# Retention plus channel mix on one core: the first q block in halves of the heads, v of block 1 ahead of its k, and a new hand order

## The chip, the core and the metric

The kernel runs on one core of a Trainium2 chip. The metric is device time in microseconds (us). Each engine of the core (PE for matmuls, DVE, ACT, POOL, and SP, which here only issues transfers) runs its own list of instructions in order and waits at semaphores for the others.

## The reference, cut to what matters

Two layers follow each other. The first is a linear recurrence for each of 4 batches and 8 heads (768 tokens, 64 values a head); the second mixes each token with the one before it and runs a gated network of three weight matrices (512x1024, 1024x512, 512x512).

```python
gamma = 1.0 - 2.0 ** (-5.0 - np.arange(H))
for t in range(S):
    state = gamma * state + einsum('bhd,bhe->bhde', k[:, :, t], v[:, :, t])
    y[:, :, t] = scale * einsum('bhd,bhde->bhe', q[:, :, t], state)
x = y.transpose(0, 2, 1, 3).reshape(B, S, H * D)
xk = mu_k * x + (1 - mu_k) * x_prev          # x_prev: x one token earlier
xr = mu_r * x + (1 - mu_r) * x_prev
k = maximum(xk @ w_k, 0); v = k * k @ w_v; r = sigmoid(xr @ w_r)
out = r * v
```

## The kernel before, in words

The tokens are cut into 12 blocks of 256 (`TM`), three to a batch; a block is two chunks `u` of 128. Heads are taken in pairs `j` (four of them). Everything is written as a string `ORDER` of words such as `S.1.0@23`: a code, its block and further numbers, and after `@` the banks of PSUM that the result goes to (eight banks, 0 to 7). The program walks through the string and emits the functions of the codes; there is no scheduler, so the string alone fixes the order of the instructions of each engine. Waits follow from the data, from the reuse of PSUM banks and from the rings of buffers (four each for q, v and k, three for the scaled k, five for the output tiles).

The codes, with the engine and the line of the profile before:

- Loads. `lq`, `lv` (POOL queue, L175; they cast to 16 bits), `lk.n` (SP queue), `lk.n.2` (POOL queue), `wk.h`, `wv.h`, `wr` (POOL queue, L510, L517, L513; a half of w_k, a half of w_v, the whole of w_r, 512 KB each as stored). `mu` loads two small vectors over ACT's queue.
- Retention. `ks` scales k (L188; `.0` on DVE, `.1` on POOL). `T` turns k (PE L203, 8 instructions); `Tq` turns q and `Tk` turns k in 32 small instructions into two banks (PE L221). `E.n.0` copies the turned q, `E.n.1` the turned k (ACT L249). `S.n.i` scores (PE L257), `M.n.i` masks them (DVE L264), `C` makes the new state (PE L282), `U` adds it up (DVE L294, L298), `G` decays it (POOL L301), `I` and `Y` make the output (PE L313, L326), `D` scales it into x (DVE L340; `Du` by chunks, L348).
- Channel mix. `dx.n.e` takes the difference to the token before (L355; e=0 on DVE, 1 on POOL); `X.n.w.j` mixes (DVE L369, w=0 for xk, 1 for xr). `K.n.g` is a quarter of the first matrix product (PE L406), `Q` squares its positive part (two ACT instructions, L413 and L416), `R.n.tb` is the gate's product (PE L420), `s` its sigmoid (ACT L426), `V.n.tb.part` half of the last product (PE L432), `O.n.tb` the output tile (DVE L438), `st.n.tb` its store (SP queue, L445).
- For block 0 the mix goes by chunks: `du`, `Xu`, `Ku` (PE L386), `Qu`. The last output tile goes by halves of its columns: `Vc` (PE L450), `Oc` (DVE L457), `sc`.
- `gy` builds a table of powers (DVE L500 to L503, eight instructions), `mt` and `me` turn and copy mu, and `z.n` is n matmuls on zeros whose result nobody reads.

As the program is built, a transfer of POOL's queue waits until the one eight places before it has landed, since the queue takes eight semaphores in turn; SP and ACT share eight more in the same way.

Of the kernel before, what the change touches and what calls it, by code (L numbers as in the profile page):

```python
# [25 lines left out]
Xu.0.1.1.2.3 s.0.0 X.1.0.3.4 R.0.1@4 E.2.1 X.1.0.2.3 X.1.0.1.2 X.1.0.0.1 Tq.2@67 s.0.1 C.2@3
X.1.1.3.4 lq.6 E.2.0 K.1.2@2 X.1.1.0.1 X.1.1.1.2 K.1.3@4 X.1.1.2.3 Q.1.2 U.2.0 G.2.0 K.1.1@5 Q.1.3
ks.3.1 S.2.0@23 I.2.0@67 M.2.0 K.1.0@4 lk.5.2 V.0.0.1 Q.1.0 lv.5 S.2.1@23 T.3.1@4 M.2.1 V.0.1.1
E.3.1 O.0.0 Y.2 Q.1.1 O.0.1 st.0.0 C.3@23 D.2 Tq.3@45 st.0.1 ks.6.1 R.1.0@0 E.3.0 U.3.0 V.1.0.0@1
U.3.1 s.1.0 G.3.1 S.3.0@23 I.3.0@45 S.3.1@67 ks.4.1 R.1.1@0 M.3.1 V.1.0.1 s.1.1 M.3.0 dx.2.1  # L30
T.4.1@0 V.1.1.0@6 O.1.0 E.4.1 st.1.0 Y.3 lk.7 lq.5 X.2.0.3.4 Tq.4@01 X.2.0.2.3 C.4@23 E.4.0
X.2.0.1.2 lv.7 V.1.1.1 X.2.0.0.1 X.2.1.2.3 lv.6 K.2.1@7 X.2.1.1.2 X.2.1.3.4 X.2.1.0.1 K.2.3@0
Q.2.1 U.4.0 D.3 G.4.0 R.2.0@7 Q.2.3 ks.5.1 K.2.0@2 U.4.1 O.1.1 s.2.0 K.2.2@3 Q.2.0 st.1.1 G.4.1
lk.10 S.4.0@67 lk.8 I.4.0@45 Q.2.2 dx.3.1 S.4.1@01 lk.9 V.2.1.0@2 M.4.1 V.2.0.0@3 M.4.0 lq.8
R.2.1@0 X.3.0.2.3 lq.7 V.2.0.1 X.3.0.1.2 s.2.1 X.3.1.0.1 V.2.1.1 X.3.1.1.2 X.3.0.0.1 X.3.1.3.4
C.5@0 Tq.5@67 X.3.0.3.4 Y.4 E.5.0 X.3.1.2.3 O.2.0 T.5.1@1 U.5.0 K.3.0@6 st.2.0 E.5.1 D.4 G.5.0
K.3.1@3 Q.3.0 O.2.1 dx.4.1 S.5.0@45 I.5.0@67 st.2.1 Q.3.1 S.5.1@01 M.5.0 K.3.3@2 M.5.1 K.3.2@3
R.3.0@4 X.4.0.3.4 Q.3.2 X.4.1.2.3 Y.5 X.4.0.0.1 Q.3.3 X.4.1.3.4 Tq.6@01 X.4.1.1.2 C.6@23 X.4.0.1.2
lq.10 E.6.0 V.3.0.0@5 U.6.0 X.4.0.2.3 D.5 T.6.1@2 R.3.1@0 E.6.1 X.4.1.0.1 V.3.0.1 U.6.1 s.3.1
G.6.1 s.3.0 S.6.0@23 I.6.0@01 ks.7.1 S.6.1@67 O.3.0 K.4.0@4 M.6.1 st.3.0 K.4.2@5 dx.5.1 M.6.0  # L40
T.7.1@6 V.3.1.0@7 E.7.1 K.4.3@2 lv.8 X.5.0.0.1 Q.4.0 X.5.1.0.1 K.4.1@6 X.5.0.1.2 Q.4.3 X.5.1.1.2
X.5.0.2.3 V.3.1.1 X.5.1.3.4 Q.4.2 C.7@23 O.3.1 Y.6 Q.4.1 U.7.0 Tq.7@45 D.6 G.7.0 R.4.1@2 E.7.0
ks.8.1 U.7.1 V.4.0.0@6 s.4.1 S.7.0@45 I.7.0@23 S.7.1@01 M.7.0 dx.6.1 V.4.0.1 M.7.1 R.4.0@7 lq.9
Tq.8@45 s.4.0 X.5.0.3.4 C.8@0 X.6.0.1.2 Y.7 E.8.0 lv.9 X.6.1.1.2 O.4.0 T.8.1@7 lv.10 K.5.3@1 D.7
st.4.0 E.8.1 st.3.1 K.5.2@6 lk.11 X.6.1.0.1 X.6.0.2.3 K.5.1@7 X.6.0.3.4 X.6.0.0.1 K.5.0@2
X.6.1.2.3 Q.5.1 X.5.1.2.3 K.6.2@7 dx.7.1 Q.5.2 V.4.1.0@3 Q.5.0 R.5.1@6 lv.11 X.7.1.1.2 Q.6.2
X.7.1.0.1 V.4.1.1 X.6.1.3.4 lq.11 X.7.1.3.4 s.5.1 K.6.1@7 Q.5.3 V.5.1.0@6 R.6.0@1 G.7.1 ks.9.1
U.8.0 K.6.0@2 s.6.0 O.4.1 V.5.1.1 st.4.1 Q.6.0 G.8.0 R.5.0@2 O.5.1 Q.6.1 X.7.0.2.3 st.5.1 S.8.0@01
I.8.0@67 S.8.1@45 M.8.0 s.5.0 V.5.0.0@3 X.7.0.3.4 T.9.1@2 M.8.1 V.5.0.1 E.9.1 V.6.0.0@0 O.5.0
X.7.0.0.1 K.6.3@1 st.5.0 X.7.0.1.2 X.7.1.2.3 Tq.9@23 Q.6.3 Y.8 C.9@45 E.9.0 D.8 R.6.1@1 V.6.0.1  # L50
U.9.0 dx.8.1 s.6.1 U.9.1 S.9.0@67 O.6.0 I.9.0@45 S.9.1@23 K.7.3@1 M.9.0 ks.10.1 R.7.0@0 Q.7.3
K.7.0@1 X.8.0.1.2 K.7.1@6 M.9.1 G.9.1 Q.7.0 R.7.1@1 X.8.1.3.4 s.7.0 X.8.0.2.3 Q.7.1 X.8.0.3.4
Tq.10@23 Y.9 X.8.0.0.1 X.8.1.2.3 C.10@67 s.7.1 T.10.1@0 E.10.0 U.10.0 K.7.2@1 G.10.0 ks.11.1
U.10.1 V.6.1.0@2 D.9 Q.7.2 V.7.0.0@1 E.10.1 G.10.1 V.7.0.1 dx.9.1 V.6.1.1 O.7.0 st.7.0 S.10.0@45
O.6.1 I.10.0@01 S.10.1@67 M.10.0 T.11.1@3 st.6.1 K.8.0@2 M.10.1 K.8.2@4 Q.8.0 X.9.0.3.4 C.11@2
Tq.11@67 E.11.1 X.9.0.2.3 Y.10 X.8.1.0.1 X.8.1.1.2 E.11.0 V.7.1.0@5 X.9.0.1.2 X.9.1.0.1 Q.8.2
V.7.1.1 X.9.0.0.1 U.11.0 D.10 K.8.3@4 G.11.0 K.8.1@2 O.7.1 Q.8.3 dx.10.1 S.11.0@01 I.11.0@45 Q.8.1
S.11.1@67 M.11.0 K.9.0@3 X.9.1.1.2 K.9.3@2 Q.9.0 X.10.1.0.1 X.9.1.2.3 R.8.0@3 M.11.1 V.8.1.0@0
X.9.1.3.4 X.10.1.2.3 Y.11 X.10.0.3.4 X.10.1.1.2 K.9.1@1 D.11 K.9.2@6 dx.11.1 R.8.1@7 Q.9.2 V.8.1.1
Q.9.3 X.11.0.2.3 V.8.0.0@6 X.11.0.1.2 s.8.0 X.10.0.2.3 V.8.0.1 Q.9.1 X.10.0.0.1 X.10.0.1.2 R.9.0@1  # L60
X.11.0.0.1 X.11.1.1.2 K.10.0@3 X.10.1.3.4 s.9.0 X.11.1.3.4 s.8.1 V.9.0.0@1 O.8.0 X.11.0.3.4 st.8.0
R.10.0@2 X.11.1.0.1 st.6.0 st.7.1 K.10.2@6 s.10.0 V.9.1.0@2 R.9.1@7 V.9.1.1 s.9.1 O.8.1 Q.10.2
K.11.1@7 O.9.1 st.8.1 K.11.2@6 X.11.1.2.3 Q.11.1 K.10.3@7 Q.10.0 R.11.1@0 Q.10.3 K.10.1@3 V.9.0.1
Q.10.1 K.11.0@7 O.9.0 Q.11.2 V.10.1.0@3 st.9.0 Q.11.0 V.10.1.1 s.11.1 R.10.1@2 V.10.0.0@0 s.10.1
V.10.0.1 K.11.3@2 O.10.0 O.10.1 R.11.0@7 st.10.0 Q.11.3 st.9.1 st.10.1 V.11.0.0@6 s.11.0 V.11.0.1
Vc.11.1.0@7 O.11.0 Vc.11.1.1@2 st.11.0 Oc.11.1.0 sc.11.1.0.0 Oc.11.1.1 sc.11.1.1.1
"""


# [1 line left out]
def kernel(  # L71
# [13 lines left out]
    B, H, S, D = q.shape  # L85
# [3 lines left out]
    C = 128  # L89
    TM = 2 * C  # L90
    NJ = H // 2
# [103 lines left out]
    def turned(n, a, j0=0):  # L195
        return banks("T", n, a, j0).bitcast(F16)
# [14 lines left out]
                            Q16(n)[:, 2 * j + hp, i * D : i * D + D], ident,  # L211
                        )

    def trans_small(n, a):
        pt = turned(n, a)[:, :, 0 : 2 * NJ * D].rearrange("p u (j i t) -> p u j i t", j=NJ, i=2)
        for j in range(NJ):
            for i in range(2):
                for u in range(2):
                    r = slice(u * D, u * D + D)
                    for hp in range(2):  # L220
                        nc.tensor.transpose(  # L221
                            pt[hp * D : hp * D + D, u, j, i, :],
                            KS(n)[r, i, 2 * j + hp] if a
                            else Q16(n)[r, 2 * j + hp, i * D : i * D + D], ident[r, r],
                        )

    def trans_q(n):
        trans_small(n, 0)

    def trans_k(n):  # L230
        trans_small(n, 1)

    def transed(n, a, j0=0, j1=NJ):
        pt = turned(n, a, j0)
        if len(BANK["T", n, a, j0]) == 2:
            pt = pt[:, :, 0 : 2 * NJ * D]
            if a == 0:
                pt = pt.rearrange("c u (j i p) -> c u j p i", j=NJ, i=2)
                out = QT(n).rearrange("c j u (p i) -> c u j p i", i=2)
            else:  # L240
                pt = pt.rearrange("c u (ji p) -> c u ji p", p=D)
                out = KT(n).rearrange("c j i (u p) -> c u (j i) p", u=2)
        elif a == 0:
            pt = pt.rearrange("c (j i p) -> c j p i", j=NJ, i=2)[:, j0:j1]
            out = QT(n)[:, j0:j1].rearrange("c j u (p i) -> c j (u p) i", i=2)
        else:
            pt = pt.rearrange("c (j i p) -> c j i p", j=NJ, i=2)[:, j0:j1]
            out = KT(n)[:, j0:j1]
        nc.scalar.copy(out=out, in_=pt)  # L249
# [279 lines left out]
    for word in ORDER.split():  # L529
        word, _, at = word.partition("@")  # L530
        code, *args = word.split(".")
        args = tuple(int(x) for x in args)
        if at:
            key = args
            if code in ("T", "Tq", "Tk"):
                code_key, key = "T", (args[0], args[1] if code == "T" else int(code == "Tk"), (args[2:] + (0,))[0])
            else:
                code_key = code
                key = {"I": args[:1], "S": args[:2] + (args[2:] + (0,))[:1]}.get(code, args)
            BANK[(code_key,) + key] = [int(x) for x in at]  # L540
        CODES[code](*args)
# [30 lines left out]
```

## Time and profile before

| | |
|---|---|
| median of 3 runs | 160.89 us (160.67 to 161.34) |
| the profiled execution | 161.76 us |
| its span (first to last instruction) | 159.5 us |
| busy, PE / DVE / ACT / POOL | 151.9 / 116.7 / 93.6 / 75.1 us |
| matmuls on zeros (L494) | 37 of 2478, 11.5 us |
| moved by DMA | 21.98 MB, read from HBM 24.25 MB |

The profile is one execution. Busy time of PE counts modelled ends of pipelined matmuls, so it says little about how much could be saved. More is seen when the work that PE has done is set against the clock: the time that is not work is what can be saved.

### The profile page before, as it was taken

What the parts mean: (1) busy time and instruction counts of PE and PEld (TensorE: products, weight loads), DVE (VectorE), ACT (ScalarE), POOL (GpSimd) and SP (SyncE); (2) the same over time, 40 slices, a digit from 0 to 9 for tenths busy, and PEclk for the clock granted to TensorE, in tenths of its full rate; (3) what the DMA queues carried; (4) which work ended last, traced back from release to release, by engine and by line L of the source; (5) the groups of instructions that cost most, each with busy time, mean ns of one, the idle gap of its engine ahead of it and who ended that gap; (6) DMA issues with size and microseconds to landing.
All of it is one profiled execution on the core that took longest, in us unless ns stands there. A gap on an engine that the chain in (4) does not pass through costs nothing.

```text
span 159.5 us, 5601 instructions
## 1 busy us (share of the span) xinstructions
PE 151.9 (95%) x2478; PEld 98.8 (62%) x2478; DVE 116.7 (73%) x209; ACT 93.6 (59%) x148; POOL 75.1 (47%) x73
## 2 busy tenths in 40 slices
PE   7899999998999999999999989999999999999991
PEld 2355676765577477677577546677586665576560
DVE  0759999849695999978795979797698959431141
ACT  3220484967349367829666955649558538199540
POOL 7963745595969614293974920292904130000000
PEclk9999999999999999999999999999999999999999
DMA  5999999999999999475159991100030000510153
GB/s 140 163 246 205 228 245 239 229 222 223 293 209 207 264 244 252 91 128 53 16 60 229 230 147 66 70 6 4 0 132 4 4 0 0 197 70 18 48 197 132
DMA packets 39543, 21.98 MB, mean 138 GB/s; under 512 B 25816, under 2 KB 35936, under 8 KB 39520
## 3 DMA queue, kind: packets, MB, share of 16 engines
q0 software_dynamic: 28320, 11.54, 54.6%
q1 hardware_dynamic: 10752, 9.83, 19.8%
q8 instruction: 19, 0.31, 0.8%
q10 hardware_dynamic: 448, 0.26, 0.6%
q14 instruction: 4, 0.03, 0.1%
HBM read 24.25 MB, written 6.29 MB: 191 GB/s over the span
## 4 chain that ended last, share of the span: by engine, by line
PE 65%; DMA 18%; DVE 7%; POOL 5%; issue 2%; POOLq 0%; DVEq 0%
PE ps L432 21%; PE ps L406 19%; PE ps L420 11%; DMA q<-in_q_dram 10%; DMA wk<-in_moe_w_k_dram 8%; DVE xr L369 4%; PE ps L257 3%; PE ps L326 3%; PE ps L203 2%; PE ps L313 2%; POOL v L175 2%; PE ps L221 2%; PE ps L282 1%; DVE xk L369 1%; POOL q L175 1%
## 5 line engine op out<-in xcount | busy, mean ns | idle before, releaser
L432 PE MATMUL ps<-wv,k 128*128 128x512 f16 x184 | 45.2, 379 | 0.1
L406 PE MATMUL ps<-xk,wk 128*128 128x256 f16 x352 | 42.6, 273 | 0.1
L406 PEld LDWEIGHTS <-wk 128*128 128x128 f16 x352 | 33.9, 98 | 7.3
L413 ACT ACTIVATE kr<-ps 128x512 f32<-128x512 f32 x44 | 25.9, 590 | 19.9 <-PE ps L406 19.9
L264 DVE TENSOR_TENSOR a<-ps,c_sb 128x1024 f16<-128x1024 f32 (+1 forms) x26 | 28.9, 1135 | 10.6 <-PE ps L257 9.4
L416 ACT ACTIVATE k<-kr 128x512 f16<-128x512 f32 x44 | 27.7, 630 | 1.4
L432 PEld LDWEIGHTS <-k 128*128 128x128 f16 x184 | 17.3, 98 | 17.8 <-issue 0.2
L355 POOL TENSOR_TENSOR dx<-xT 128x1024 f32<-128x1024 f32 x10 | 18.9, 1890 | 19.1 <-DVE xT L340 15.7
L438 DVE SCALAR_TENSOR_TENSOR os<-ps,rs 128x512 f32<-128x512 f32 x23 | 15.6, 685 | 16.8 <-PE ps L432 9.5
L369 DVE SCALAR_TENSOR_TENSOR xr<-dx,mu,xT 128x256 f16<-128x256 f32 (+1 forms) x52 | 25.3, 518 | 2.1 <-POOL dx L355 2.1
L420 PE MATMUL ps<-wr,xr 128*128 128x512 f16 x96 | 24.8, 379 | 0.5 <-DVE xr L369 0.5
L369 DVE SCALAR_TENSOR_TENSOR xk<-dx,mu,xT 128x256 f16<-128x256 f32 (+1 forms) x52 | 22.9, 478 | 3.0 <-POOL dx L355 3.0
L426 ACT ACTIVATE rs<-ps 128x512 f32<-128x512 f32 x24 | 14.0, 591 | 12.2 <-PE ps L420 12.1
L301 POOL TENSOR_TENSOR tg<-t,csm_sb 128x256 f16<-128x256 f32 x16 | 10.0, 623 | 23.4 <-DVE t L298 23.3
L188 POOL TENSOR_TENSOR ks<-k,csm_sb 128x1024 f16<-128x1024 f32 x9 | 17.1, 1898 | 2.1 <-PE ps L282 2.1
L249 ACT COPY kT<-ps 128x1024 f16<-128x1024 f16 (+1 forms) x13 | 12.3, 944 | 9.7 <-PE ps L203 9.4
L249 ACT COPY qT<-ps 128x1024 f16<-128x1024 f16 x12 | 12.1, 1006 | 5.4 <-PE ps L221 5.4
L175 POOL DMA_DIRECT2D q<-in_q_dram x12 | 11.0, 918 | 8.2 <-PE ps L282 4.4
L420 PEld LDWEIGHTS <-xr 128*128 128x128 f16 x96 | 9.0, 98 | 9.4 <-DVE xr L369 1.0
L340 DVE TENSOR_TENSOR xT<-ps,gy_sb 128x1024 f32<-128x1024 f32 x11 | 13.4, 1217 | 1.1 <-PE ps L326 0.9
L494 PE MATMUL ps<-zero 128*128 128x512 f16 x37 | 11.5, 451 | 1.2 <-DVE xT L478 1.2
L175 POOL DMA_DIRECT2D v<-in_v_dram x12 | 10.8, 902 | 2.4 <-DMA wk<-in_moe_w_k_dram 1.1
(43 smaller groups left out, 137.1 us busy)
## 6 DMA issues: line engine op xcount, KB each, us to landing
out_dram<-os SPq DMA_DIRECT2D x23, 256.0 KB, 2.4
q<-in_q_dram POOLq DMA_DIRECT2D x12, 256.0 KB, 9.2
v<-in_v_dram POOLq DMA_DIRECT2D x12, 256.0 KB, 9.0
k<-in_k_dram SPq DMA_DIRECT2D x6, 512.0 KB, 11.3
k<-in_k_dram POOLq DMA_DIRECT2D x5, 512.0 KB, 13.4
wk<-in_moe_w_k_dram POOLq DMA_DIRECT2D x2, 512.0 KB, 11.9
wv<-in_moe_w_v_dram POOLq DMA_DIRECT2D x2, 512.0 KB, 16.0
k<-in_k_dram SPq DMA_DIRECT2D x2, 256.0 KB, 3.6
```

The source lines that it names most:

```text
L175: eng.dma_start(out=d(n)[:, 2 * j0 : 2 * j1], in_=rows(x, n)[:, 2 * j0 : 2 * j1])
L188: (nc.vector, nc.gpsimd)[e].tensor_tensor(out=KS(n)[:, :, h0:h1], in0=K32(n)[:, h0:h1].rearrange("p h (i d) -> p i h d", i=2), in1=gks[:, ...
L249: nc.scalar.copy(out=out, in_=pt)
L264: nc.vector.tensor_tensor(out=A2(n)[:, i, :, j0:j1], in0=pairs(banks("S", n, i, j0))[:, :, j0:j1], in1=causal[:, i, None, None, :].to_broa ...
L355: (nc.vector, nc.gpsimd)[e].tensor_tensor(out=DX(n)[:, j0:j1, t0:t1], in0=x[:, j0:j1, c + t0 : c + t1], in1=x[:, j0:j1, c - 1 + t0 : c - 1 ...
L369: nc.vector.scalar_tensor_tensor(out=XM[w](n)[:, j, t0:t1], in0=DX(n)[:, j, t0:t1], scalar=mu[:, w * NCO + j : w * NCO + j + 1], in1=x[:, ...
L406: nc.tensor.matmul(pz[:, i, :], lhsT=wk16[:, co, fo * P : fo * P + P], rhs=XM[0](n)[:, co, :], start=(i == 0 and co == 0), stop=(co == NCO ...
L413: nc.scalar.activation(out=kr, in_=banks("K", n, g).rearrange("p (i t) -> p i t", i=2), func=AF.Relu)
L416: nc.scalar.activation(out=K2(n)[:, 2 * g : 2 * g + 2], in_=kr, func=AF.Square)
L420: nc.tensor.matmul(banks("R", n, tb), lhsT=XM[1](n)[:, co, tb * P : tb * P + P], rhs=wr16[:, co, :], start=(co == 0), stop=(co == NCO - 1),)
L432: nc.tensor.matmul(banks("V", n, tb, 0), lhsT=K2(n)[:, fo, tb * P : tb * P + P], rhs=wv16[:, fo, :], start=(fo == 0), stop=(fo == NFO - 1),)
L438: nc.vector.scalar_tensor_tensor(out=OS(2 * n + tb), in0=banks("V", n, tb, 0), scalar=1.0 / (KSC * KSC), in1=RS(2 * n + tb), op0=ALU.mult, ...
```

## The change

Block 0's q is loaded, turned, copied and scored in two halves of the heads; `trans_small` and `transed` get bounds `j0`, `j1` for that. v of block 1 goes ahead of k of block 1 and between the halves of q. `ks.1` goes from DVE to POOL. `ks.6`, `ks.8`, `ks.11` and `dx.4`, `dx.6`, `dx.7`, `dx.8`, `dx.11` go from POOL to DVE. k of blocks 6 and 7 goes from SP's queue to POOL's. k of blocks 7, 8, 10 and 11 is turned by `Tk` in place of `T`. The matmuls on zeros go from 37 to 28, and all other words are in a new order with new banks. No other arithmetic is added or taken away.

```diff
 ORDER = """
-lk.0.0.2.4 lk.0.0.0.2 lq.0 lv.0 lv.1 lk.1.2 ks.0.0.2.4 lq.1 ks.0.0.0.2 wk.1 gy z.10@1 T.0.1.0.2@0
-T.0.1.2.4@1 E.0.1.0.2 wk.0 mu wr z.4@4 Tq.0@23 E.0.1.2.4 lk.2.2 E.0.0 wv.0 z.5@4 S.0.0.0.2@23
-S.0.0.2.4@01 C.0@45 M.0.0.0.2 U.0.0 lq.2 M.0.0.2.4 z.2@6 I.0.0@23 S.0.1.0.2@67 U.0.1 S.0.1.2.4@01
-M.0.1.0.2 G.0.1 M.0.1.2.4 ks.1.0 z.5@4 Y.0 Du.0.0 z.1@4 C.1@01 mt@6 U.1.0 T.1.1@2 Du.0.1 G.1.0 me
-Tq.1@45 lv.2 du.0.0.1 du.0.0.0 E.1.0 lk.3.2 Xu.0.1.1.1.2 Xu.0.1.1.0.1 E.1.1 Xu.0.0.1.0.1 wv.1
...
+lk.0.0.0.2 lk.0.0.2.4 lq.0.0.2 lv.0 lq.0.2.4 lv.1 lk.1.2 mu gy ks.0.0.2.4 ks.0.0.0.2 z.11@1
+T.0.1.0.2@0 T.0.1.2.4@1 Tq.0.0.2@23 E.0.1.0.2 E.0.1.2.4 E.0.0.0.2 mt@4 z.3@5 S.0.0.0.2@23 C.0@01
+M.0.0.0.2 U.0.0 U.0.1 lq.1 wk.0 wk.1 wv.0 G.0.1 wr ks.1.1 Tq.0.2.4@67 E.0.0.2.4 z.2@5 I.0.0@67
+S.0.0.2.4@23 M.0.0.2.4 S.0.1.0.2@01 M.0.1.0.2 z.1@5 S.0.1.2.4@23 M.0.1.2.4 z.4@5 Y.0 Du.0.1 z.3@5
+C.1@23 Du.0.0 du.0.0.1 me T.1.1@7 E.1.1 Tq.1@01 E.1.0 z.4@5 S.1.0@01 du.0.0.0 Xu.0.0.1.3.4
+Xu.0.0.0.1.2 Xu.0.0.1.0.1 Xu.0.0.1.1.2 Xu.0.0.1.2.3 Ku.0.0.1@7 U.1.0 wv.1 lq.2 lk.2.2 G.1.0 M.1.0
+Xu.0.0.0.2.3 Xu.0.0.0.0.1 Xu.0.0.0.3.4 I.1.0@45 S.1.1@01 Ku.0.1.1@2 M.1.1 Xu.0.1.1.1.2
+Xu.0.1.0.1.2 Xu.0.1.1.0.1 Xu.0.1.1.2.3 Xu.0.1.0.0.1 Xu.0.1.0.2.3 Xu.0.1.1.3.4 Xu.0.1.0.3.4
+Ku.0.0.0@6 Ku.0.1.0@0 Qu.0.1.1 Qu.0.0.1 Qu.0.0.0 Y.1 lv.2 lk.3.2 lq.3 lk.4.2 lk.5.2 V.0.1.0@2
+V.0.0.0@1 R.0.1@6 R.0.0@7 V.0.1.1 D.1 dx.1.0 X.1.0.3.4 X.1.0.1.2 X.1.0.2.3 X.1.0.0.1 X.1.1.2.3
+U.1.1 lq.5 G.1.1 lv.3 K.1.3@4 K.1.2@3 s.0.1 s.0.0 Qu.0.1.0 Q.1.3 K.1.0@0 Tq.2@45 Q.1.2 E.2.0
+ks.2.0 C.2@3 T.2.1@7 E.2.1 Q.1.0 V.0.0.1 X.1.1.1.2 O.0.1 X.1.1.3.4 X.1.1.0.1 R.1.0@2 s.1.0 U.2.0
...
+V.2.1.0@3 T.6.1@0 V.2.1.1 R.2.1@1 V.2.0.1 lk.10 st.0.0 lv.7 dx.3.1 M.5.0 X.3.0.3.4 X.3.0.0.1
+X.3.0.1.2 X.3.0.2.3 X.3.1.0.1 K.3.0@4 K.3.1@5 U.4.0 G.4.0 O.2.0 E.6.1 s.2.1 U.4.1 O.2.1 Q.3.0
+Q.3.1 ks.7.1 G.4.1 I.4.0@67 C.5@4 S.4.1@23 M.4.1 X.3.1.1.2 X.3.1.3.4 X.3.1.2.3 K.3.3@1 K.3.2@5
...
+dx.6.0 X.6.0.1.2 X.6.1.2.3 X.6.1.1.2 X.6.0.2.3 X.6.1.3.4 X.6.0.0.1 X.6.0.3.4 Q.5.0 E.9.0 R.5.1@5
+s.5.1 E.9.1 R.5.0@6 K.5.3@5 Q.5.3 V.5.1.0@7 s.5.0 V.5.0.0@5 V.5.0.1 K.6.1@6 Q.6.1 U.7.0 st.4.0
...
-    def trans_small(n, a):
-        pt = turned(n, a)[:, :, 0 : 2 * NJ * D].rearrange("p u (j i t) -> p u j i t", j=NJ, i=2)
-        for j in range(NJ):
+    def trans_small(n, a, j0, j1):
+        pt = turned(n, a, j0)[:, :, 0 : 2 * NJ * D].rearrange("p u (j i t) -> p u j i t", j=NJ, i=2)
+        for j in range(j0, j1):
...
-    def trans_q(n):
-        trans_small(n, 0)
+    def trans_q(n, j0=0, j1=NJ):
+        trans_small(n, 0, j0, j1)
...
-                pt = pt.rearrange("c u (j i p) -> c u j p i", j=NJ, i=2)
-                out = QT(n).rearrange("c j u (p i) -> c u j p i", i=2)
+                pt = pt.rearrange("c u (j i p) -> c u j p i", j=NJ, i=2)[:, :, j0:j1]
+                out = QT(n)[:, j0:j1].rearrange("c j u (p i) -> c u j p i", i=2)
```

## The prediction

> **What bounds the kernel now.** I read the page first, for which engine is full, when, and at what clock.
>
> ```profile
> PE 151.9 (95%) x2478; PEld 98.8 (62%) x2478; DVE 116.7 (73%) x209; ACT 93.6 (59%) x148; POOL 75.1 (47%) x73
> PEclk9999999999999999999999999999999999999999
> PE 65%; DMA 18%; DVE 7%; POOL 5%; issue 2%; POOLq 0%; DVEq 0%
> ```
>
> PE is nearly always busy, at a full granted clock. How much of that is work? The chain of waits shows back-to-back rates, because its pieces end where the next begins (start, length, what).
>
> ```profile
> 6.53 12.81 DMA wk<-in_moe_w_k_dram
> 22.17 16.05 DMA q<-in_q_dram
> 38.27 0.44 PE ps L221 x32
> ...
> 85.99 0.10 issue
> 86.09 1.90 POOL dx L355
> 88.02 4.52 DVE xr L369 x3
> ...
> 143.15 0.86 PE ps L420 x4
> ...
> 149.22 1.73 PE ps L432 x8
> ...
> 154.41 1.76 PE ps L450 x16
> ```
>
> An `R` or half a `V` is 0.865, a `K` 0.873 (16 matmuls in 1.75), a `Ku` 1.0, a `T` 0.45, a `Tq` 0.385, an `S` 0.35, a `C` 0.38 (0.22 in a batch's last block), `I` 0.2 to 0.3, `Y` 0.62 to 0.72. Over all words without `z`: K 44x0.873 + Ku 4.0 + V 46x0.865 + Vc 1.76 + R 24x0.865 + 33.8 of retention and `mt` = 138.6 us. PE's last matmul ends at 156.15, so about 17.5 us of PE are no work. I set clock against work done, word by word (start minus work before it = loss): first `Ku` 19.22 - 5.05 = 14.2; `K.1.2` 29.5 - 14.3 = 15.2; after the wait for q of block 3, 38.64 - 22.4 = 16.2; `S.7.0` 77.76 - 61.4 = 16.4; `K.6.0` 92.81 - 75.5 = 17.3; end 17.4. So the loss is 14 us of start, 2 us of arrivals, 1.2 us of one stall from 78 to 93, and nothing after. That last stall, in the timeline of DVE and of POOL:
>
> ```profile
> 88.02 4.90 DVE L369 SCALAR_TENSOR_TENSOR xr<-dx,mu,xT 128x256 f16<-128x256 f32 x4 [2.08 <-POOL dx L355]
> ```
>
> ```profile
> 89.75 0.63 POOL L301 TENSOR_TENSOR tg<-t,csm_sb 128x256 f16<-128x256 f32 x1
> 90.32 1.91 POOL L188 TENSOR_TENSOR ks<-k,csm_sb 128x1024 f16<-128x1024 f32 x1
> ```
>
> Four `X` take 0.4 each elsewhere (1.66 for four); here 4.90, and they end only after POOL's `ks` has. An `M`, `D` or `O` beside POOL keeps its time (L264 at 78.30, two in 2.36, beside `dx` on POOL).
>
> **The change part by part.** The profiled execution took 161.76, 2.26 more than its span; the median of the runs is 0.87 lower. I take the same difference off both.
>
> *Work.* Four `T` become `Tk`, 4x(0.385-0.45) = -0.26. Nine `z` fewer cost and gain nothing: they fill PE's idle time at the start.
>
> *Arrivals.* POOL's queue lands in the order of issue. Before: q0 7.93, v0 9.35, v1 10.84, k1 12.53, q1 13.77, half of w_k 16.73, the other 19.34, w_r 21.9, k2 23.4, half of w_v 25.7, q2 27.1, v2 28.65, k3 30.2, other half of w_v 33.7, v3 36.8, q3 38.2. A weight piece takes 2.3 to 3.0, a q, v or k 1.25 to 1.7. The last two gaps (3.5, 3.0) are longer: SP's k6 is on its way from 24.65 to 35.96. In the new order k6 waits behind the rest, so I space by 2.5 and 1.5: half of q0 7, v0 8.6, q0 9.4, v1 10.8, k1 12.5, q1 13.8, w_k 16.7 and 19.3, w_v 21.9, w_r 24.4, w_v 26.7, q2 28.1, k2 29.6, v2 31.1, k3 32.6, q3 34.1, k4 35.6, k5 37.1, q5 38.5, v3 40. The queue stays full though POOL now holds w_r behind `G.0.1` and the next pieces behind `ks.1.1` until 14.4: what was issued before lasts to 24.
>
> *A transfer in two halves.* The row is k0 on SP: its two 256 KB halves landed at 4.06 and 5.12, the second 1.06 later, so I charge a half no second start, only POOL's issue (0.9 at most, before any wait). The Trainium skill, DMA: Bandwidth & Descriptors, Anatomy of one DMA — SWDGE (gpsimd) path, gives each DMA a fixed part of about 2.0 us beside its bytes; if that came in series, the sum would be up to 2.0 worse. The halves of k0 do not show it.
>
> *The start.* `gy` now precedes `ks.0` on DVE: 3.3 to 5.3, then the two `ks` to 6.65; before, the second ended at 5.83, so `T.0` is 0.8 late. Turn, copy (0.53 a half), score: `S.0.0.0.2` at 9.0 (9.54 before), `C.0` 9.2, `M`, `U`, `U` to 10.75, then three `M` of 0.62 to 12.8; `Y.0` ends at 13.5 (13.90). DVE no longer has `ks.1` in between (1.14): four `Du`/`du` of 0.62 and five `Xu` of 0.27 from 13.7 end at 17.55. Beside it k1 12.53 + `ks.1.1` on POOL 1.86 + `C.1` 0.38 + `T.1` 0.45 + two copies of 0.92 and latencies = 17.5 for `S.1.0`. First `Ku` at 17.9 with 4.4 done: loss 13.5, 0.7 better. Then w_k's second half (19.3) and `M.1.0`: `Ku.0.1.1` 19.75, three more, `Y.1`, `V.0.1.0` at 23.5 (26.03 before) with 9.8 done: 13.7 against 14.9. `R.0.1` at 25.25 has w_r (24.4), `V.0.1.1` at 27.0 has w_v (26.7), `C.2` waits to 31.3 for v2, and adding on, `Y.2` starts at 37.3 with 23.1 done: 14.2. The q of block 3, which cost 0.67, has been there for 3 us.
>
> *From there to the end.* POOL's five `dx` and two more `ks` than it gains go to DVE: 7x1.14 = 8.0 us of DVE work. After 38 us DVE has 88 us to do in about 105, so it can hide if each `X` is ready for its `K`. Adding words up on DVE and PE (D 1.13, M 1.14, X 0.395, U 0.34, O 0.6) leaves before the first `K` of blocks 4, 6, 7, 8, 11: 1.3, 0.75, 1.35, 0.9, 1.35 us. The stall of 78 to 93 (1.2) has no successor: no `X` stands beside a POOL `ks`, `dx` or `G` in this sum; those fall beside `M`, `D`, `O` or in waits. What is late next are ties of ACT (`Q.5.3` before `V.5.0.0`, `Qu.0.0.0` before `V.0.0.0`) at 0.1 to 0.3 each; I allow 0.6. Loss at the end 14.8 against 17.4. The tail is the same: last tile, half store, 3.3.
>
> The Trainium skill, SBUF — State Buffer, Who interferes with whom, says that a DVE instruction with two inputs in SBUF and a POOL instruction that reads SBUF block each other. By it also a `ks` or `dx` moved to DVE could stand up to 1.86 longer; no row here shows that pair, and in my sum none meet.
>
> Sum: -2.6 - 0.26, with 0.2 kept back for latencies: about -2.6. Profiled 159.2, median 158.3.
>
> **The rivals.**
>
> *DVE becomes the bound (slower).* For: 8.0 us more on it, and margins of 0.75 to 1.35. If an `X` meets a POOL instruction it costs what the row shows, 4.90 - 1.66 = 3.2; that uses up one margin and passes about 2 us on to PE, and all later POOL work moves against DVE as well. It decides once DVE is more than 0.75 late at `K.6`; two such meetings or half of the 8.0 exposed give +4.0 - 2.8 = +1.2: 162.1. Against: DVE keeps waiting for PE (`D` after `Y`, `O` after `V`), which takes up lateness.
>
> *The first stores come late (less gain).* SP's queue now has k10 ahead of `st.0.0`, and k10 waits for `ks.6` on DVE (about 50.6). `O.2.1` takes the buffer that `st.0.0` empties, 6.5 later; `S.4.1` needs the bank that `O.2.1` reads, and all PE stands behind `S.4.1`. The DMA view has, for single issues of SP at 24.65, 37.03, 49.93:
>
> ```profile
> k<-in_k_dram SPq DMA_DIRECT2D x1, 512.0 KB, 11.3
> out_dram<-os SPq DMA_DIRECT2D x1, 256.0 KB, 7.9
> out_dram<-os SPq DMA_DIRECT2D x1, 256.0 KB, 6.0
> ```
>
> With 6.0, no wait; with 7.9, 1.4 late, 159.7. I take 6.0, the one with a k just ahead.
>
> *The start gives nothing (no change).* k1 lands 1 to 1.5 later or `ks.1.1` holds up w_v; `S.1.0`, and later `V.0.1.1`, move with it, and the 2.0 of arrivals is gone. Left: 1.2 + 0.26 less 0.8 allowed, 0.6: 160.3. Nor do the halves of q help where `gy` has made k late: that is in the sum already.
>
> **How the numbers follow.** A measurement tells about 0.5%, 0.8 us, from no change. Forecast 0.57 (its own range 157.4 to 159.4: no allowance at all, or 1.1 more); late stores 0.16, also faster; no gain 0.09; DVE bound 0.18. Faster 0.73, same 0.09, slower 0.18. The range goes to 161.2: that leaves out most of the slower case, some 0.15, and 0.05 below 157.4.
>
> **What would show it.** Right: first `Ku` (then L387) near 17.9, no PE wait for q of block 3, last matmul near 153.5, no `X` of over 1 us. Wrong: first `Ku` after 19, a wait of PE for `O` near 58 (late stores), waits of PE on `X` from 65 to 125, or DVE busy over 95% there.

## The result, and the profile after

The changed kernel is slower: 163.57 us median (163.34 to 164.65, 4 runs) beside 161.12 for the kernel before on the same chip, a ratio of 1.016 with a 95% interval of 1.013 to 1.019. The forecast was 158.3, faster. The profiled execution took 163.34 with a span of 161.6. (Medians below are over all runs of a kernel; ratios leave out disturbed runs, so the two can differ.) One correction to the title and the description of the change: v of block 1 precedes its k in either order, and what stands between the halves of q is v of block 0.

Page of the changed kernel: busy time, the granted clock in 40 slices, and the shares of the chain.

```profile
PE 151.8 (94%) x2565; PEld 98.1 (61%) x2565; DVE 121.9 (75%) x216; ACT 93.7 (58%) x149; POOL 64.5 (40%) x69
...
PEclk9999999999999995999999999999999999999998
...
PE 73%; DVE 10%; DMA 9%; ACT 3%; issue 2%; POOL 1%; SPq 0%; DVEq 0%; POOLq 0%
```

One slice of the clock row reads 5 (60.6 to 64.6 us), where the row of before has only nines. The chain of waits leads through that place (start, length, what), and here it passes through a store of the output:

```profile
49.65 1.14 DVE ks L189
51.23 9.04 DMA out_dram<-os
61.66 3.34 PE ps L407 x16
```

Timeline of SP (its queue), then of DVE, then of PE, around it:

```profile
50.81 0.37 SPq L176 DMA_DIRECT2D k<-in_k_dram  x1
51.23 0.58 SPq L446 DMA_DIRECT2D out_dram<-os  x1
```

```profile
60.37 0.69 DVE L439 SCALAR_TENSOR_TENSOR os<-ps,rs 128x512 f32<-128x512 f32 x1 [2.76 <-DMA out_dram<-os]
```

```profile
61.11 0.54 PE L258 MATMUL ps<-qT,kT 64*64 64x128 f16 x14 [2.63 <-DVE os L439]
61.59 3.40 PE L407 MATMUL ps<-xk,wk 128*128 128x256 f16 x16
```

`lk.10` leaves SP when `ks.6` is done (50.8), `st.0.0` leaves 0.4 later and lands 9.04 later, `O.2.1` on DVE waits 2.76 for its buffer, `S.4.1` on PE waits 2.63 for `O.2.1`. Then two `K`, 1.75 elsewhere, take 3.40. The windows view (PE busy, PEld, DVE, ACT, POOL, the granted clock, DMA share, GB/s; the DMA share counts overlapping packets, so it passes 1) gives the reason for the last step:

```profile
58.30:61.50 3.20, 0.57 (x22) 0.34 (x15) 0.69 (x1) 1.07 (x2) 1.28 (x2) 0.96 1.27 280
61.50:65.00 3.50, 3.50 (x29) 2.32 (x28) 2.74 (x5) 1.23 (x2) 0.48 (x1) 0.55 1.08 378
65.00:68.00 3.00, 3.00 (x82) 1.85 (x83) 1.87 (x2) 2.71 (x5) 1.77 (x3) 1.00 0.23 87
```

Set against the work done, as in the prediction, the loss is 14.9 us when PE stops at 58.2; 17.9 when it goes on; 18.7 and 19.5 after the two slow `K`; 19.4 to 19.6 from there to the end. So nearly all of the surprise lies in seven microseconds: 2.6 of waiting, some 0.3 around it, and 1.6 at half clock.

### The profile page after: what moved, and what is told of

Its sections match the earlier page's. It is cut to its first block, busy times and chain, and to the rows that moved or that the text cites. A ratio compares the mean times of both kernels' runs of the same rounds, so it can differ in the third digit from the quotient of the medians.

```text
span 161.6 us, 5767 instructions
## 1 busy us (share of the span) xinstructions
PE 151.8 (94%) x2565; PEld 98.1 (61%) x2565; DVE 121.9 (75%) x216; ACT 93.7 (58%) x149; POOL 64.5 (40%) x69
## 4 chain that ended last, share of the span: by engine, by line
PE 73%; DVE 10%; DMA 9%; ACT 3%; issue 2%; POOL 1%; SPq 0%; DVEq 0%; POOLq 0%
PE ps L407 22%; PE ps L433 21%; PE ps L421 12%; DMA out_dram<-os 6%; DMA q<-in_q_dram 4%; PE ps L258 4%; DVE a L265 3%; PE ps L327 3%; PE ps L314 3%; PE ps L222 3%; DVE xk L370 2%; PE ps L283 1%; PE ps L204 1%; ACT k L398 1%; PE ps L451 1%
## 5 line engine op out<-in xcount | busy, mean ns | idle before, releaser
L407 PE MATMUL ps<-xk,wk 128*128 128x256 f16 x352 | 44.6, 279 | 0.0
L433 PE MATMUL ps<-wv,k 128*128 128x512 f16 x184 | 44.2, 379 | 0.1
L421 PE MATMUL ps<-wr,xr 128*128 128x512 f16 x96 | 23.6, 379 | 0.0
L370 DVE SCALAR_TENSOR_TENSOR xk<-dx,mu,xT 128x256 f16<-128x256 f32 (+1 forms) x52 | 21.3, 460 | 2.8 <-POOL dx L356 2.6
L370 DVE SCALAR_TENSOR_TENSOR xr<-dx,mu,xT 128x256 f16<-128x256 f32 (+1 forms) x52 | 21.7, 458 | 0.1
L356 POOL TENSOR_TENSOR dx<-xT 128x1024 f32<-128x1024 f32 x5 | 9.5, 1891 | 27.5 <-DVE xT L341 27.5
L258 PE MATMUL ps<-qT,kT 64*64 64x128 f16 x384 | 11.5, 222 | 3.7 <-DVE os L439 2.6
L189 POOL TENSOR_TENSOR ks<-k,csm_sb 128x1024 f16<-128x1024 f32 x7 | 13.2, 1898 | 0.6 <-DMA k<-in_k_dram 0.5
L250 ACT COPY qT<-ps 128x1024 f16<-128x1024 f16 (+1 forms) x13 | 12.2, 943 | 1.5 <-PE ps L222 1.4
L176 POOL DMA_DIRECT2D q<-in_q_dram x13 | 11.5, 888 | 2.5 <-DMA wv<-in_moe_w_v_dram 1.6
```

Of the source, the lines that this page charges most:

```text
L176: eng.dma_start(out=d(n)[:, 2 * j0 : 2 * j1], in_=rows(x, n)[:, 2 * j0 : 2 * j1])
L258: nc.tensor.matmul(pa[u * D : u * D + D, hp, j, :], lhsT=KT(n)[r, j, i, u * D : u * D + D], rhs=QT(n)[r, j, u, :], start=(j == j0), stop=( ...
L370: nc.vector.scalar_tensor_tensor(out=XM[w](n)[:, j, t0:t1], in0=DX(n)[:, j, t0:t1], scalar=mu[:, w * NCO + j : w * NCO + j + 1], in1=x[:, ...
L407: nc.tensor.matmul(pz[:, i, :], lhsT=wk16[:, co, fo * P : fo * P + P], rhs=XM[0](n)[:, co, :], start=(i == 0 and co == 0), stop=(co == NCO ...
L421: nc.tensor.matmul(banks("R", n, tb), lhsT=XM[1](n)[:, co, tb * P : tb * P + P], rhs=wr16[:, co, :], start=(co == 0), stop=(co == NCO - 1),)
L433: nc.tensor.matmul(banks("V", n, tb, 0), lhsT=K2(n)[:, fo, tb * P : tb * P + P], rhs=wv16[:, fo, :], start=(fo == 0), stop=(fo == NFO - 1),)
```

## The experiments

Lines in the codes' helpers differ by one between kernels (the string of words has one line more or less); words, not lines, identify an instruction below. Times of the runs:

| run | median us | ratio to before, 95% |
|---|---|---|
| e1, four stores ahead of k of block 10 | 160.61 | 0.993 to 0.998 |
| e2, six output tiles | 161.14 | 0.997 to 1.002 |
| e3, zeros in the wait | 162.17 | 1.005 to 1.009 |
| e4, before, k of block 6 later | 161.34 | 0.998 to 1.002 |
| e5, one store ahead | 159.56 | 0.988 to 0.993 |
| e6, e5 and loads spread | 159.61 | 0.988 to 0.993 |
| e7, before, q in halves alone | 160.76 | 0.996 to 1.001 |
| e8, e5 with q whole | 159.99 | 0.989 to 0.994 |
| e9, changed kernel, loads spread alone | 160.61 | 0.993 to 0.998 |
| e10, e5 with records shifted | 163.36 | 1.003 to 1.010 |
| e11, e6 and dx.3 on DVE | 159.94 | 0.987 to 0.993 |
| e12, e11 and two loads moved | 160.94 | 0.996 to 1.001 |

### e1: the first stores ahead of k of block 10

```diff
-V.2.0.1 lk.10 st.0.0 lv.7
+V.2.0.1 st.0.0 st.0.1 st.1.0 st.1.1 lk.10 lv.7
-lk.9 st.2.0 st.0.1 st.1.0 st.1.1 st.2.1
+lk.9 st.2.0 st.2.1
```

> The changed kernel with the first four stores (st.0.0 to st.1.1) ahead of k of block 10 in SP's list, nothing else moved. Theory (the first store stands behind k10, its buffer comes free late, O.2.1 and S.4.1 wait, and PE's clock drops after the pause): the wait at 58.3 to 61.1 and the slow K.3.3 and K.3.2 go, the loss of PE stays at about 15 from 58 us to the end as before that place, and the median falls by about 4.5 us, to 159.1 with the kernel before at 161.1 (ratio 0.987). Rival (DVE is the bound of blocks 3 to 8 in any case, and the store only happened to come last): DVE or POOL holds PE up some places later, the loss climbs again to over 17, and the time is 161.5 or more.

Measured 160.61 (159.56 to 161.32). The wait in `S.4.1` and the half clock are gone, so the late store was their cause. But the time is 1.5 above the expectation: the loss climbs to over 17, as the rival said, though not by DVE or POOL. The profiled run, the slowest of the twelve, has stops inside groups of small matmuls, which the view calls "issue" because no semaphore explains them. Timeline of PE:

```profile
38.15 0.53 PE L327 MATMUL ps<-a,v 64*64 64x128 f16 x23 [0.34 <-issue]
44.63 0.25 PE L283 MATMUL ps<-v,ks 64*64 64x64 f16 x7 [0.46 <-issue]
52.20 0.47 PE L327 MATMUL ps<-a,v 64*64 64x128 f16 x19 [1.18 <-issue]
```

### e2: six output tiles in place of five

```diff
-    OS = ring("os_", 5, [dm], F32)
+    OS = ring("os_", 6, [dm], F32)
```

> The changed kernel with six output tiles in place of five, SP's list as in the changed kernel. Theory (what costs is the buffer that O.2.1 waits for, not the traffic of k10, k8 and k9 itself): O.2.1 takes a fresh tile, st.0.0 still lands near 60 us, and the time is that of the kernel with the stores first, 159.1. Rival (the burst of transfers at 50 to 66 us slows something else, k or v or DVE): over 160.5.

With six tiles `O.10.1` comes to lie on the tile of `O.7.1`, which the order stores later, so 128 rows of the output differ; the amount of work is the same. Measured 161.14, on the rival's side of 160.5 and not the theory's 159.1. Still there is no wait in `S.4.1`: the buffer was what `O.2.1` waited for. PE's last matmul ends at 154.94, 3.2 before the changed kernel's; part of it is given back at the end, where the late stores now stand in the way (4.1 us from the last matmul to the end of the span, 3.5 otherwise). A stop named issue of 0.74 stands at 70.95. That the traffic slows something else as well is not excluded.

### e3: matmuls on zeros in the wait

```diff
-C.5@4 S.4.1@23
+C.5@4 z.14@0 S.4.1@23
```

> The changed kernel with 14 matmuls on zeros into a free bank ahead of S.4.1, so that PE works while it waits for O.2.1 (14 x 0.216 = 3.0 us). Theory (the clock drops because PE pauses for 2.6 us): the wait stays, the granted clock stays at 1.0, K.3.3 and K.3.2 take 0.87 each and not 1.7, and the median falls by 1.6 us to about 162.0. Rival (the clock drops at that time whatever PE does, say by the traffic or by the load of the other engines): 163.6, and K.3.3 still takes 1.7.

Measured 162.17, 1.4 below the changed kernel, with the same wait. Timeline of PE and the windows of this run:

```profile
58.11 3.20 PE L495 MATMUL ps<-zero 128*128 128x512 f16 x14
61.24 0.42 PE L258 MATMUL ps<-qT,kT 64*64 64x128 f16 x16
61.59 1.92 PE L407 MATMUL ps<-xk,wk 128*128 128x256 f16 x16
```

```profile
61.50:65.00 3.50, 3.50 (x103) 2.72 (x92) 3.14 (x6) 2.27 (x5) 0.47 (x1) 1.00 1.07 372
```

`S.4.1` comes at the same time, the two `K` take 1.92 instead of 3.40, the clock stays at 1.00. The half clock was the price of PE's pause, not of the `K` or of the transfers beside them (the DMA share is 1.07 and 1.08).

### e4: the kernel before, with k of block 6 loaded later

```diff
-lk.6 T.2.1@3
+T.2.1@3
-st.0.1 ks.6.1 R.1.0@0
+st.0.1 lk.6 R.1.0@0
...
-ks.5.1
+ks.5.1 ks.6.1
```

> The kernel before with k of block 6 moved in SP's list from ahead of the first store to behind st.0.1, and its scaling on POOL behind ks.5.1. Theory of the arrivals (k6 takes its share of the transfers from 28 to 35 us): w_v's second half, v3 and q3 land 1.5 to 2.5 us earlier, the 0.67 us wait of PE for q3 goes, the loss after it is 15.4 in place of 16.2, median 160.3 against 161.1. Rival (POOL's queue sets its own pace and k6 costs it nothing): no change, 161.1.

Measured 161.34, no difference. The wait of `Tq.3` for q of block 3 (0.67 before) is gone, as the theory of arrivals has it, but waits at `Ku.0.0.1`, `T.2.1` and `S.5.0` grew by about as much (0.3, 0.4, 0.4). Removing this one wait was worth nothing, since the next ones stood some 0.5 us behind it.

### e5, e6: one store ahead; the loads spread as well

```diff
 e5, from the changed kernel:
-V.2.0.1 lk.10 st.0.0 lv.7
+V.2.0.1 st.0.0 lk.10 lv.7
 e6, from e5:
-lk.7.2 lq.6 lq.8 G.3.1 lq.7 lq.9 S.4.0@23
+lk.7.2 lq.6 G.3.1 S.4.0@23
-lk.10 lv.7 dx.3.1
+lk.10 lv.7 lq.7 dx.3.1
-G.5.0 D.4
+G.5.0 lq.8 lq.9 D.4
```

> The changed order with one swap: the first store of the output is issued on SP ahead of k of block 10; the other three of the first two blocks stay behind it. With all four ahead (the first run) the time was 160.6, and TensorE stopped inside groups of small matmuls: 1.18 us in Y.3, 0.46 in C.3, 0.34 in Y.2. All such stops lie at the same place of every 256 records of TensorE (record 189 of each 256), and each ends 2.3 to 2.8 us after a 16 KB packet of instructions starts to move. Theory A: the stops are TensorE waiting for its own instructions, and the early stores made them long: their packets at 38 to 40, 42 to 44 and 49 to 50 us go beside the loads on the 16 engines, and the packet of instructions that started at 46.96 in the changed kernel started at 49.62. Then with one store ahead it starts at 46.5 to 47.5, Y.3 has no stop, and the time is 159.6 (160.6 less 1.2, plus a little for later stores). Theory B: the loads of GpSimd's queue alone make the packets late (the queue is full from 45 to 54 us in either): 160.6 as in the first run. Theory C: there is nothing but spread between executions: 160.0 to 160.6, with a stop of another length.

> The run before it in this call, and q of blocks 7, 8 and 9 loaded later: 7 behind v of block 7 (some 51 us), 8 and 9 behind G.5.0 (some 63 us), in place of with k of block 6 at 44 us. Theory B (the full queue of GpSimd makes instruction packets late): no stop of TensorE over 0.3 us from 38 to 60, and 159.0 to 159.4. Theory A (only the early stores do): within 0.3 of the run before it, 159.4 to 159.8. A rival against both: v of block 7 or q of blocks 8 and 9 land late, C.7 or Tq.8 waits, and the time is 160.5 or more.

e5 measured 159.56: two words exchanged take 4.0 us off the changed kernel and make it 1.0% faster than the kernel before (0.7 to 1.2%). Timeline of PE in e5:

```profile
38.40 0.53 PE L326 MATMUL ps<-a,v 64*64 64x128 f16 x23 [0.35 <-issue]
44.60 0.25 PE L282 MATMUL ps<-v,ks 64*64 64x64 f16 x7 [0.18 <-issue]
51.34 0.47 PE L326 MATMUL ps<-a,v 64*64 64x128 f16 x19 [0.36 <-issue]
```

The stop in `Y.3` fell from 1.18 to 0.36, with the packet of instructions starting at 48.67 (49.62 in e1, 46.96 in the changed kernel). The time is theory A's, the mechanism only half of it: the packet is not as early as A said, and in e6, with the queue relieved too, it started at 47.35 and `Y.3` has no stop (one of 0.40 in `Y.2` stays). How much the early stores hold this packet up is not settled: it starts 2.7 to 3.1 us after PE passes the place of the stop before it (near 44 us) in four runs without an early store, 2.2 to 4.1 after in five with one, 5.0 after in e1; e10, where these places differ, is left out. The part of the loads shows at the next place, near 50 us: 3.4 to 4.2 in the six runs that load q of blocks 7 to 9 at 44 us, 0.7 to 1.2 in the four that spread them (e6, e9, e11, e12). e6 is not faster for that: 159.61, since `dx.3` now stood behind two loads on POOL and PE lost 0.6 at `K.3.1` and `I.4.0`.

### e7, e8: the halves of q, alone and undone

```diff
 e7, from the kernel before:
-lq.0 lv.0
+lq.0.0.2 lv.0 lq.0.2.4
-Tq.0@23 E.0.1.2.4 lk.2.2 E.0.0 wv.0 z.5@4 S.0.0.0.2@23 S.0.0.2.4@01 C.0@45 M.0.0.0.2 U.0.0 lq.2 M.0.0.2.4 z.2@6
+Tq.0.0.2@23 E.0.1.2.4 lk.2.2 E.0.0.0.2 wv.0 z.3@4 S.0.0.0.2@23 C.0@45 M.0.0.0.2 Tq.0.2.4@67 E.0.0.2.4 U.0.0 lq.2 z.2@6 S.0.0.2.4@01 M.0.0.2.4
 e8, from e5:
-lq.0.0.2 lv.0 lq.0.2.4
+lq.0 lv.0
-Tq.0.0.2@23 E.0.1.0.2 E.0.1.2.4 E.0.0.0.2
+Tq.0@23 E.0.1.0.2 E.0.1.2.4 E.0.0
-Tq.0.2.4@67 E.0.0.2.4 z.2@5
+z.2@5
```

> The kernel before with one part of the change alone: q of block 0 loaded, turned and scored in halves of the heads, all else in its old order. If the halves are worth what the prediction gave them: the first score starts at 8.6 instead of 9.5, the first Ku some 0.9 earlier, and the time is 160.3. If q of block 1 and the weights hold the start, which the halves don't move: the first score comes at 8.6, S.1.0 still starts at 18.4, and the time stays at 161.2. The other order of all pieces would then be what brought the first Ku to 17.9.

> The first run of this call with the halves undone: q of block 0 in one load, one turn and one copy, in the new order. If the halves carry the start: first score 9.5, first Ku 18.8, time 0.9 above the first run of this call (160.5 if that is 159.6). If the new order carries it: first Ku within 0.3 of 17.9, and the time within 0.3 of that run.

Timeline of PE in e7, first score and first `Ku`, then the same two in e8:

```profile
8.44 0.31 PE L257 MATMUL ps<-qT,kT 64*64 64x128 f16 x8
...
18.58 1.27 PE L386 MATMUL ps<-xk,wk 128*128 128x128 f16 x16
```

```profile
9.00 0.31 PE L257 MATMUL ps<-qT,kT 64*64 64x128 f16 x8 [0.42 <-ACT qT L249]
...
17.93 1.07 PE L386 MATMUL ps<-xk,wk 128*128 128x128 f16 x16
```

In the old order the halves bring the first score 1.1 forward (9.54 to 8.44) and the first `Ku` 0.6 (19.22 to 18.58; 18.95 in e4, which also has the old start), between the two expectations; the time, 160.76, cannot be told from before. In the new order, without the halves, the first `Ku` still comes at 17.93 (17.74 in e5, 17.55 to 18.11 in the nine runs with that start and the halves). The time is 0.4 above e5, more than the 0.3 expected, with intervals that overlap. The new order, not the halves, carries the start.

### e9: the loads spread alone, the store still behind k of block 10

The edits of e6 on the changed kernel, with `lk.10 st.0.0` left as they are.

> The changed kernel with its stores in its own order (the first one behind k of block 10 on SP), and q of blocks 7, 8 and 9 loaded later, as in the second run of the last call. The prediction priced the late first store at 6.0 to 7.9 us and it took 9.04 (51.23 to 60.27), in a stretch in which GpSimd's queue is full until 55 us. If the full queue made it late: with three loads fewer in that stretch (768 KB, some 4 us of the queue) the store lands by 56 to 57.5, O.2.1 (57.6) does not wait, TensorE does not stop in S.4.1, and the time is 159.7 to 160.2. If the store takes its 9 us whatever the loads do: S.4.1 starts at 60 to 61 and the time is 163.4.

Measured 160.61; 0.4 above the upper end of the first expectation and 2.8 below the second. The DMA view of the two issues on SP, in the changed kernel and in e9 (KB each, us from issue to landing):

```profile
k<-in_k_dram SPq DMA_DIRECT2D x1, 512.0 KB, 8.5
out_dram<-os SPq DMA_DIRECT2D x1, 256.0 KB, 9.0
```

```profile
k<-in_k_dram SPq DMA_DIRECT2D x1, 512.0 KB, 4.4
out_dram<-os SPq DMA_DIRECT2D x1, 256.0 KB, 5.9
```

Windows view from 50 to 55 us, the changed kernel and e9:

```profile
50.00:55.00 5.00, 5.00 (x108) 3.08 (x104) 4.09 (x6) 2.13 (x3) 2.76 (x2) 1.00 1.76 194
```

```profile
50.00:55.00 5.00, 5.00 (x108) 3.13 (x108) 3.37 (x4) 2.26 (x4) 3.71 (x3) 1.00 0.77 143
```

Same place in SP's queue, almost the same issue time (51.2 and 51.4), but the DMA share beside it is 0.77 instead of 1.76, and both transfers land 3 to 4 us sooner. `O.2.1` does not wait. So it took both to make PE wait, the store behind k of block 10 and POOL's loads beside the two: with either one taken away (e5, e9) the wait is gone. e9 is still 1.0 slower than e6, which has the same loads and the first store ahead; in the profiled executions most of that is a stop named issue in `Y.5` (0.71 at 71.11) which e6 does not have.

### e10: every record of PE 120 places further on

```diff
-z.11@1
+z.7@1 y.64@56
+    def tiny(count):
+        for n in range(count):
+            r, c = slice(n % 2 * D, n % 2 * D + D), slice(n // 2 % 2 * D, n // 2 % 2 * D + D)
+            nc.tensor.matmul(
+                banks("y", count)[c, n % 2, 0:D], lhsT=zero[r, 0:D], rhs=zero[r, 0:D],
+                start=True, stop=True, skip_group_check=True,
+            )
```

> The swap of the first store (159.56), with four of the eleven matmuls on zeros at the start replaced by 64 tiny ones on zeros (64x64 by 64 columns) in the same wait: TensorE's work on the data is as it was, but every later record is 120 places further on. Theory: TensorE gets its own instructions in packets of 256 records; the next packet starts to move 0.9 us after TensorE enters the last one where the queues are empty (from 70 us on) and 3.1 to 4.1 us after where they are full (38 to 55), and is of use 2.3 to 2.8 us later. The borders then move with the count, to records that ran at some 43.7, 47.1 and 52.7 us; the packet entered at 43.7 is used up in 3.5 us, so TensorE stops at some 47 us, in the scores around S.4.0, for 2 to 3 us, once more for up to 1 at 53 to 56, and no longer in Y.2, C.3 and Y.3 (0.9 in all): time 161.0 to 162.5. Rival: the stops belong to those groups (their operands, their banks): they stay in Y.2, C.3 and Y.3, and the time is 159.6.

Measured 163.36, ratio 1.003 to 1.010, which is 161.5 to 162.7 beside the 161.07 of before: 2 to 3 us slower than e5, with nothing added after the start. Of that 0.6 is the start itself: the granted clock falls to 0.59 at 7 to 9 us, behind the tiny matmuls and a pause of 1.81 us after them, and `S.1.0` starts at 18.02 (17.39 in e5). The profiled run is the fastest of them (161.34). Its only stop named issue:

```profile
86.34 0.35 PE L221 MATMUL ps<-c_sb,q 64*64 64x64 f16 x19 [1.92 <-issue]
```

The groups `Y.2`, `C.3` and `Y.3` no longer stop, so the stops do not belong to them; the new one, in `Tq.9`, again begins at record 189 of a block of 256, 2.39 after a packet started. The place was missed: at 42.5, where I expected 3 to 4 us of delay, the engines were less busy (DMA share 0.75) and the packet started 0.02 after the border; at 81.3 (share 1.30) it took 2.65 to start and 2.39 more to be of use, and the 256 records lasted 3.1. The profile is one execution, so where the slower ones lose more is not seen.

### e11, e12: towards a better version

```diff
 e11, from e6:
-D.3 V.2.0.0@2
+D.3 dx.3.0 V.2.0.0@2
-lq.7 dx.3.1 M.5.0
+lq.7 M.5.0
 e12, from e11:
-lv.7 lq.7 M.5.0
+lv.7 lq.7 lq.8 M.5.0
-ks.7.1 G.4.1
+ks.7.1 G.4.1 lq.9
-G.5.0 lq.8 lq.9 D.4
+G.5.0 D.4
```

> The swap of the first store with the loads spread (159.61), and the difference of block 3 (dx.3) moved from GpSimd to VectorE, right behind D.3 and ahead of M.5.0. In that run VectorE stood idle for 1.59 us ahead of X.3.0 because dx.3 on GpSimd ran from 52.81 to 54.72, behind two loads; TensorE then waited 0.27 at K.3.1 and 0.36 at I.4.0. On VectorE dx.3 runs beside nothing that waits, from 52.0 to 53.1; M.5.0 moves to 54.3, X.3.0 starts at 54.3 instead of 54.76. Expected 159.0 to 159.3, with both waits gone; 159.6 if the 0.6 us is taken up by the next chain.

> The run with dx.3 on VectorE (159.94), and q of blocks 8 and 9 moved once more: in that run they were issued at 61.9 and 62.8, with v of blocks 6 and 8 right behind them, GpSimd's queue was full from 65 to 70, the packet of instructions that TensorE needed at 69.7 started at 68.66, and TensorE stopped in Y.5 for 1.28 us. Here q of block 8 goes behind q of block 7 (52 us), in the gap in which GpSimd otherwise does nothing, and q of block 9 behind G.4.1 (59 us). If the late packet of instructions is what that run lost: no stop over 0.4 us in Y.5, and 159.0 to 159.4. If the stop only moves to another border of 256 records: 159.6 to 160.0, with a stop named issue of about 1 us at another record 189 of 256. A price that both allow: the first stores land later again behind q of block 8, and O.2.1 waits: 160.5 or more.

e11 measured 159.94. The wait at `K.3.1` is gone, that at `I.4.0` down to some 0.2, and the loss at 64.5 us is 14.9 (15.6 in e6; but 0.5 of the difference is there at 51 us, where the orders are still the same). PE then stops 1.28 us in `Y.5`, and the time is above both expectations. e12, meant to cure that, measured 160.94. Timeline of PE in e12:

```profile
37.75 0.53 PE L326 MATMUL ps<-a,v 64*64 64x128 f16 x23 [0.21 <-issue]
44.22 0.25 PE L282 MATMUL ps<-v,ks 64*64 64x64 f16 x7 [0.45 <-issue]
71.79 0.41 PE L326 MATMUL ps<-a,v 64*64 64x128 f16 x15 [1.28 <-issue]
```

The stop in `Y.5` stayed. From 37.75 to 71.79 PE passes six borders of 256 records, and at five of them it stands still (0.42, 0.64, 0.31, 0.25 and 1.50 between the starts of the two instructions). The median went past the rival's 160.0 too, and `O.2.1` does not wait, so the price named there is not the reason. Why it is 1.0 above e11 stays open: in the profiled executions all of the difference (0.8) arises before 52 us, where the two orders are the same. That the supply of instructions takes what other waits give up would fit, but is not shown.

## Why the prediction was wrong, point by point

*The start and the arrivals: right.* First `Ku` 17.88 (17.9 forecast), `V.0.1.0` 23.26 (23.5), `Y.2` 37.11 (37.3), the loss there 14.0 (14.2). PE does not wait for q of block 3 (landed at 33.88, turned at 36.83). The order in which POOL's queue lands held within about half a microsecond. Charging the halves of q no second start was right too: the second half was turned at 9.36, where the list had it land at 9.4. The fixed part of about 2.0 us that the Trainium skill, DMA: Bandwidth & Descriptors, Anatomy of one DMA — SWDGE (gpsimd) path, gives each DMA did not come in series. What the prediction did not separate is that the halves themselves give little (e7, e8).

*DVE does not become the bound: right.* Its busy time rose by 5.2 to 121.9, less than the 8.0 that were moved, since the `X` took 47.7 in all and not 51.8; the longest takes 0.49. PE waits for nothing over 0.15 us from 65 to 125 us, and the loss is flat from 65 us to the end.

*The late first stores: the failed step.* The mechanism is in the prediction as its second rival, with its place near 58 us, and the term was mis-sized. The prediction took 6.0, so no wait, from the row "with a k just ahead", and 7.9, a wait of 1.4, as the upper end. Measured: 9.04, a wait of 2.63. The row of 6.0 was misread. Timeline of SP in the kernel before:

```profile
44.81 0.39 SPq L175 DMA_DIRECT2D k<-in_k_dram  x1
49.93 0.33 SPq L445 DMA_DIRECT2D out_dram<-os  x1
```

That k had left 5.1 us before its store; here k of block 10 leaves 0.4 us before. In the three pairs read here the store lands behind the k: 2.2 us behind before (53.66 and 55.88), 1.0 in the changed kernel (59.28 and 60.27), 1.9 in e9 (55.36 and 57.29). By these rows the price was what the k still had to go, 8.5 us beside POOL's full queue and 4.4 in e9; the k of 44.81 had taken 8.85, which was the nearer row. What the store would take at 51 us with no k ahead no run shows; in e1 one that left at 45.11 without took 7.65. The prediction's list of arrivals ends at 40 us, so POOL's load at 51 was not in the price either (DMA share from 50 to 55 us: 1.49 before, 1.76 in the changed kernel). And a wait of PE was priced at its length. This one of 2.63 us also cost the clock, another 1.6 (1.4 in e3).

*The sum again.* Loss forecast 14.8, measured 19.6. Of the 4.8: 4.5 are the wait with its surroundings and the two slow `K`, 0.4 the stop in `Y.2`. The part outside the span was 0.5 less than before's (1.8 against 2.26). 159.2 + 4.8 - 0.5 = 163.5; the profiled run took 163.34.

*What is left without the store.* e5 took 159.56 against 158.3. Its loss is 16.2 at the end, 1.4 more than forecast; stops named issue are 0.9 of that. That is a second term that the prediction did not have at all: PE's own instructions. The rest, some 0.5, is spread over small waits, beyond what I had allowed for them.

*The chances.* Of the 0.73 for faster, 0.16 was the late store itself, counted as a smaller gain, and 0.57 a forecast that needs the store in time. Both signs hung on one price, read from two rows.

## What to carry to other kernels

Here the same two transfers took 8.5 and 9.0 us beside a DMA share of 1.76, 4.4 and 5.9 beside 0.77. So price a transfer by what stands ahead of it in its queue and by the load of the new order, and treat the longest row of the old order as no bound. In an in-order queue, put the store that frees a buffer ahead of a load that waits for something else, even if the load seems urgent. When a hand order is made denser, count instructions too: small matmuls can be used up faster than they are delivered. And compare single profiles with care: with the same words, the first `Ku` came at 17.55 to 18.11.

## What the runs showed of the hardware that was not expected

**PE waits for its instructions.** In all runs of the new order the stops named issue lie at the same record of every 256 (189 by the order of starts, matmuls and weight loads together), and resume 2.2 to 2.8 us after a 16 KB packet of the kind "instruction" starts to move; e5's page counts them:

```profile
q8 instruction: 20, 0.33, 0.8%
```

20 packets for 5130 records is some 256 each. How long after such a place (a border) the next packet starts goes with the DMA load, as e6 and e9 showed near 50 us. In e5, from the trace:

```
border passed at         31.58  38.40  44.60  51.34  59.19  65.39  70.32  74.56
next packet starts after  4.27   3.95   4.07   3.39   3.18   2.45   0.97   0.95
```

Windows view of e5, the stretch before the packet of 48.67 and the microsecond after the borders at 70.3 and 74.6 (the DMA share is the last number but one):

```profile
45.00:48.60 3.60, 3.60 (x75) 3.01 (x63) 3.33 (x8) 3.48 (x6) 2.95 (x4) 1.00 1.35 287
70.40:71.40 1.00, 1.00 (x46) 0.88 (x37) 1.00 (x3) 0.97 (x2) 0.00 (x0) 1.00 0.06 17
74.60:75.60 1.00, 1.00 (x24) 0.83 (x14) 0.99 (x4) 0.00 (x0) 1.00 (x2) 1.00 0.08 16
```

An estimate from these rows: beside full queues 256 records last at least some 6.5 us (4.0 + 2.5), beside empty ones some 3.5 (1.0 + 2.5). It varies with the packet: in the changed kernel one started 3.2 after its border, and the 256 records lasted 5.8 without a stop. An order that packs `T`, `S`, `C`, `I` and `Y` together asks for less than that. The Trainium skill, Runtime: NRT & Kernel Launch, Instruction fetch mechanics, describes blocks of 256 instructions, fetched one ahead, and calls the cost mostly hidden. The blocks agree with these runs; that it is hidden does not, where DMA is full: 1.92 us in one stop of e10. That a packet is asked for as the border is passed is inferred from the times: in the loaded stretch none starts before its border is executed, later some start up to 1.5 us ahead. The trace does not show the request.

**A pause of PE cost its clock.** After 2.63 us without a matmul the granted clock was 0.55 on average from 61.5 to 65.0 us; with zeros in the pause it stayed at 1.00 (e3). In e10 a pause of 1.81 us right behind the tiny matmuls was followed by 0.59 from 7 to 9 us, while pauses of 1.91 at the start of e11 and 1.92 at 86 us in e10 were not followed by a fall; these runs give no threshold. The Trainium skill, TensorE: Matmul & The Clock Gate, HAM oscillation — how this bites in real kernels, tells of waits for DMA that lower the clock; its Part 1 puts the idle time at about 3.4 us, and here 2.6 were enough, in the one case of such length.
